# Loading one weight matrix in another order of partitions: a source walked as 16 sets of rows instead of 128 rows

## The chip, the cores and the metric

The kernel runs on one core of a Trainium2 chip. The metric is the device time of one execution in microseconds (us). A run over 1.5% above the fastest of its kernel would be called slow.

The names used: HBM is the large memory, SBUF the on-chip memory, whose leading axis is 128 partitions. PE (TensorE) multiplies matrices, DVE is the vector engine, and SyncE and ScalarE issue loads. The 16 DMA engines that carry the loads are meant wherever the text says that an engine reads or writes rows.

## The reference

Two independent problems, A and B, of the same shape, each one step of attention for a decoder with a cache. The results are put side by side.

```python
B, Sq, D = 2, 1, 576;  Hq, Hkv, Sk, Dh = 32, 16, 16384, 128      # bf16 throughout
W = min(4096, max(256, Sk // 4))                                  # 4096: the window
q = (x @ wq).reshape(B, Sq, Hq, Dh)          # wq is 576 x 4096, 4.72 MB
k, v = the last W rows of k_cache, v_cache   # 2 x 16 x 4096 x 128 each, 33.6 MB each
o = softmax(q k^T * Dh**-0.5) v
out = o.reshape(B, Sq, Hq * Dh) @ wo
```

Almost all of the work is reading 153 MB from HBM. wq of A, which the change touches, is 3% of it.

## The kernel before

The kernel holds wq in SBUF as 128 partitions of 18,432 elements (36,864 B), and partition p holds piece p of the flat matrix. Nine half rows of wq lie in one piece, so x has to be spread over the partitions in the same way: element i of x that belongs to a half row goes to the partition that holds that half row. The DVE does this with 32 x 32 transposes. The matmuls then contract over the partitions, and the order of the partitions does not matter as long as wq and x agree.

```python
wq_dma = {}
for P in range(NPROB):
    def f_wq(e, P=P):
        src = probs[P][3].rearrange("a b -> (a b)").rearrange("(p f) -> p f", p=128)
        return e.dma_start(ringf[:, P * QW:(P + 1) * QW], src).then_inc(wq_sem[P], 16)
    wq_dma[P] = dma_op("sp", wq_sem[P], 1, f_wq, [], "wq%d" % P)
# ... (cut) in turn_x(P):
    def f_xT(e, P=P):
        for k in range(4):
            last = e.transpose(xU[32 * k:32 * k + 32, P, :, 4 * P:4 * P + 32],
                               xs[:, P * 2 * D:(P + 1) * 2 * D].rearrange("p (c t) -> p t c", t=NU)[:, :, 32 * k:32 * k + 32])
# ... (cut) the matmuls of A wait for wq_dma[0] and the transposes; the caches are loaded behind wq:
    src = src_t[b, 4 * g:4 * g + 4, Sk - W:Sk, :].rearrange("k (r j) d -> r k j d", j=KJ)   # 32 x 4 rows of 32,768 B
    e.dma_start(ring[:, r, c0 * 128:c1 * 128], src[:, :, c0:c1, :].rearrange("r k j d -> r k (j d)"))
```

SyncE issues all the large loads in one order: wq of A, wq of B, then the caches into a ring of four slots, and wo among the caches. The load of wq of A is the first thing in this queue. (The small loads of x are issued by ScalarE.)

Of the kernel before, what the change touches and what calls it, by code (L numbers as in the profile page):

```python
# [62 lines left out]
def build_kernel(nc, probs, out):  # L63
# [5 lines left out]
    Bb, _one, D = x0.shape  # L69
# [18 lines left out]
    NU = (2 * D) // 128  # L88
    QW = NU * UW
# [3 lines left out]
    with es:  # L93
# [50 lines left out]
        ringf = ring[:].rearrange("p r f -> p (r f)")  # L144
# [3 lines left out]
        xU = pTf[:, 0:XW].rearrange("p (g u w) -> p g u w", g=NPROB, u=NU)  # L148
# [3 lines left out]
        xs = xt[0:32, 1, 0:NPROB * 2 * D]  # L152
# [8 lines left out]
        wq_sem = [sem("wq%d" % P) for P in range(NPROB)]  # L161
# [7 lines left out]
        def dma_op(eng, sem_h, n_dmas, fn, deps, tag):  # L169
            op = S.add(eng, fn, deps, tag)  # L170
            dma_count[sem_h] = dma_count.get(sem_h, 0) + 16 * n_dmas
            op.dma = (sem_h, dma_count[sem_h])
            return op
# [9 lines left out]
        wq_dma = {}  # L183
        for P in range(NPROB):
            def f_wq(e, P=P):
                src = probs[P][3].rearrange("a b -> (a b)").rearrange("(p f) -> p f", p=128)
                return e.dma_start(ringf[:, P * QW:(P + 1) * QW], src).then_inc(wq_sem[P], 16)
            wq_dma[P] = dma_op("sp", wq_sem[P], 1, f_wq, [], "wq%d" % P)

        pool = lambda fn, deps, tag: S.add("pool", fn, deps, tag)  # L190
# [30 lines left out]
        def turn_x(P):  # L221
            d_xs = dve(lambda e, P=P: e.tensor_tensor(xs[0:4, P * 2 * D:(P + 1) * 2 * D].rearrange("p (i t) -> p i t", t=2),  # L222
                                                      x4[:, P, :].unsqueeze(2).broadcast_to([4, D, 2]),
                                                      hmask[:, 0:2].unsqueeze(1).broadcast_to([4, D, 2]), ALU.mult),
                       [x_dma[P], d_hm, p_zx], "xs%d" % P)

            def f_xT(e, P=P):
                for k in range(4):
                    last = e.transpose(xU[32 * k:32 * k + 32, P, :, 4 * P:4 * P + 32],
                                       xs[:, P * 2 * D:(P + 1) * 2 * D].rearrange("p (c t) -> p t c", t=NU)[:, :, 32 * k:32 * k + 32])  # L230
                return last
            d_xT.append(dve(f_xT, [d_xs, p_zxU], "xT%d" % P))

# [520 lines left out]
        for op in order:  # L754
            have = seen[op.eng]
            need = {}
            for d in op.deps:
# [3 lines left out]
                k = id(s_h)  # L761
# [62 lines left out]
```

## Time and profile before

| | before |
|---|---|
| time, median of 2 | 363.21 us |
| DMA queue busy, of 16 engines' span | 98.7% |
| PE, DVE busy | 66%, 60% |
| mean rate | 424 GB/s |
| one wq row (36,864 B) on one DMA engine | 1.364 us, 27.0 GB/s |

From the profile's page of the kernel before: the busy tenths of PE and of the DMA engines and the rate in 40 slices of 9 us, and the share of the queue.

```profile
PE   0497787666485747662596675567776875668695
...
DMA  8999999999999999999999999999999999999996
GB/s 327 457 435 406 460 408 446 424 431 438 417 453 408 457 404 428 444 431 431 435 420 444 417 449 410 440 431 438 424 442 412 449 417 429 435 435 431 417 412 256
...
q1 hardware_dynamic: 6196, 153.10, 98.7%
```

DMA never falls below 9 tenths between the first slice and the last, at about 430 GB/s: the time is the bytes. The next busiest engine, PE, stands at 66%. So a microsecond lost or won in the queue at the start should move the end by about a microsecond.

From the timeline of the kernel before (start, duration, engine, what; in brackets the idle time ahead and what ended it): the issues of the first loads, the transposes of x and the first matmuls on A's and on B's wq.

```profile
0.80 0.39 SPq L187 DMA_DIRECT2D ring<-in_A_wq_dram  x1
1.25 0.41 SPq L187 DMA_DIRECT2D ring<-in_B_wq_dram  x1
...
9.63 2.78 DVE L229 STREAM_TRANSPOSE pT<-xt 32x288 bf16<-32x288 bf16 x4
...
14.20 0.61 PE L279 MATMUL ot<-ring,pT 128*32 128x512 bf16 x1 [14.20 <-DMA ring<-in_A_wq_dram]
...
25.07 0.39 PE L279 MATMUL ot<-ring,pT 128*32 128x512 bf16 x1 [0.79 <-DMA ring<-in_B_wq_dram]
```

A's wq is there at 14.2 us and B's at 25.1 us, 10.9 us later. A's x is turned by 12.4 us, so PE waits for the load and not for x.

The trace also holds one record per DMA packet, here a row of wq: its start and how long it took. It doesn't say which engine moved it. Taking the 256 wq rows in the order of their start, sixteen at a time (sixteen are in flight in 164 of 174 instants, one every 0.1 us, so I take a turn as one row per engine), the first turn takes 1.97 us on average, the second 1.37, and all others 1.364.

### The profile page before, as it was taken

Reading aid. Unit: us, or ns where it says so; the run is one execution under the profiler, and the core shown is the slowest. Engines: PE = TensorE matmul, PEld = TensorE weight load, DVE = VectorE, ACT = ScalarE, POOL = GpSimd, SP = SyncE. Lnnn points to the kernel's source line nnn. Section 1 sums busy time; section 2 is a strip of 40 time slices with the busy share of each in tenths; the row PEclk is TensorE's granted clock in tenths of the full one; section 3 lists DMA queues with packets and bytes.
Section 4 is the critical chain, followed back from the end, with each engine's and each line's share of the span. In section 5 each row is a group of like instructions: output and inputs, shape, how many; then the busy total and the mean of one; then the engine's idle time right before and its main releaser. Section 6 shows DMA issues by size and latency. Waiting matters only on the chain.

```text
span 361.8 us, 2625 instructions
## 1 busy us (share of the span) xinstructions
PE 240.2 (66%) x1292; PEld 57.2 (16%) x927; DVE 218.7 (60%) x150; ACT 46.0 (13%) x78; POOL 24.3 (7%) x84
## 2 busy tenths in 40 slices
PE   0497787666485747662596675567776875668695
PEld 0000111112111201111121121112112121112222
DVE  1901898495929591934909585682927776674622
ACT  1002100040023000500005000500005000500500
POOL 4200101100010001000010000100010001000000
PEclk9999698969988996888788796888688796868969
DMA  8999999999999999999999999999999999999996
GB/s 327 457 435 406 460 408 446 424 431 438 417 453 408 457 404 428 444 431 431 435 420 444 417 449 410 440 431 438 424 442 412 449 417 429 435 435 431 417 412 256
DMA packets 6227, 153.26 MB, mean 424 GB/s; under 512 B 700, under 2 KB 840, under 8 KB 1224
## 3 DMA queue, kind: packets, MB, share of 16 engines
q1 hardware_dynamic: 6196, 153.10, 98.7%
q8 instruction: 8, 0.13, 0.1%
q14 instruction: 3, 0.02, 0.0%
q10 hardware_dynamic: 20, 0.01, 0.0%
HBM read 153.10 MB, written 0.00 MB: 423 GB/s over the span
## 4 chain that ended last, share of the span: by engine, by line
DMA 48%; DVE 26%; PE 16%; issue 8%; ACT 1%; POOL 0%; SPq 0%
DMA ring<-in_B_k_cache_dram 17%; DVE xt L433 16%; DMA ring<-in_A_k_cache_dram 13%; DMA ring<-in_B_v_cache_dram 9%; DMA ring<-in_B_wq_dram 7%; PE st L264 5%; PE st L459 5%; DMA wob<-in_B_wo_dram 3%; PE pj L264 2%; DVE oR L566 2%; DVE mx L467 2%; DVE pT L506 2%; DVE tmp L559 2%; PE ot L536 2%; PE pj L618 1%
## 5 line engine op out<-in xcount | busy, mean ns | idle before, releaser
L459 PE MATMUL st<-xt,zq 128*128 128x512 bf16 x256 | 124.1, 485 | 86.1 <-DVE xt L433 86.1
L433 DVE STREAM_TRANSPOSE xt<-ring 128x4096 f32<-128x4096 f32 x32 | 141.5, 4427 | 28.0 <-DMA ring<-in_A_k_cache_dram 18.8
L264 PE MATMUL st<-xt,zq 128*128 128x512 bf16 x256 | 122.7, 479 | 0.0
L497 ACT ACTIVATE pR<-st,bias 128x512 bf16<-128x512 f32 x32 | 40.0, 1414 | 222.9 <-DVE bias L490 222.9
L459 PEld LDWEIGHTS st<-xt,zq 128*128 128x128 bf16 x256 | 29.4, 115 | 210.1 <-issue 107.7
L536 PE MATMUL ot<-ring,pT 128*32 128x512 bf16 x512 | 32.6, 396 | 3.9 <-DMA ring<-in_B_v_cache_dram 3.9
L490 DVE SCALAR_TENSOR_TENSOR bias<-vmask,tb,offm 128x4 f32<-128x4 f32 x8 | 1.8, 223 | 43.0 <-PE tb L487 43.0
L520 DVE TENSOR_REDUCE ssum<-tb 128x2 f32<-128x8 f32 x8 | 1.3, 162 | 36.0 <-PE tb L517 36.0
L425 POOL TENSOR_TENSOR zq<-qs,bmask 128x64 bf16<-128x64 bf16 x32 | 8.7, 293 | 168.1 <-PE st L264 145.8
L506 DVE STREAM_TRANSPOSE pT<-pR 128x2048 bf16<-128x2048 bf16 x8 | 18.4, 2303 | 0.8 <-ACT pR L497 0.7
L279 PE MATMUL ot<-ring,pT 128*32 128x512 bf16 x18 | 7.6, 421 | 15.0 <-DMA ring<-in_A_wq_dram 14.2
L559 DVE SCALAR_TENSOR_TENSOR tmp<-ot,rsb,dmask 128x512 f32<-128x512 f32 x16 | 11.5, 719 | 7.9 <-PE ot L536 7.9
L566 DVE TENSOR_REDUCE oR<-tmp 128x128 f32<-128x512 f32 x15 | 15.6, 1042 | 0.5
L536 PEld LDWEIGHTS ot<-ring,pT 128*32 128x32 bf16 x512 | 12.4, 99 | 19.6 <-DMA ring<-in_B_v_cache_dram 5.5
L618 PE MATMUL pj<-wob,oM 128*2 128x288 bf16 x48 | 12.7, 299 | 0.0
L264 PE MATMUL pj<-wob,oM 128*2 128x288 bf16 x48 | 12.7, 299 | 0.0
L264 PE MATMUL pj<-ring,pT 128*32 128x512 bf16 x36 | 11.9, 416 | 0.0
L467 DVE TENSOR_REDUCE mx<-st 128x2 f32<-128x1024 f32 x8 | 9.7, 1213 | 0.1
L497 ACT ACTIVATION_READ_ACCUMULATOR pR<-st,bias 128x1 f32 x32 | 8.8, 276 | 0.0
L264 PE MATMUL st<-ring,pT 128*32 128x512 bf16 x18 | 7.3, 407 | 0.0
L222 DVE TENSOR_TENSOR xt<-xt,hmask 4x1152 bf16<-4x1152 bf16 x2 | 2.7, 1349 | 6.7 <-DMA xt<-in_A_x_dram 6.7
L469 POOL TENSOR_TENSOR mv<-mx,v 128x2 f32<-128x2 f32 x8 | 1.6, 195 | 75.8 <-DVE mx L467 75.8
(68 smaller groups left out, 75.6 us busy)
## 6 DMA issues: line engine op xcount, KB each, us to landing
ring<-in_A_k_cache_dram SPq DMA_DIRECT2D x8, 4096.0 KB, 24.3
ring<-in_A_v_cache_dram SPq DMA_DIRECT2D x8, 4096.0 KB, 29.9
ring<-in_B_k_cache_dram SPq DMA_DIRECT2D x8, 4096.0 KB, 27.0
ring<-in_B_v_cache_dram SPq DMA_DIRECT2D x7, 4096.0 KB, 29.8
ring<-in_A_wq_dram SPq DMA_DIRECT2D x1, 4608.0 KB, 13.3
ring<-in_B_wq_dram SPq DMA_DIRECT2D x1, 4608.0 KB, 23.8
wob<-in_A_wo_dram SPq DMA_DIRECT2D x2, 2304.0 KB, 28.3
wob<-in_B_wo_dram SPq DMA_DIRECT2D x1, 2304.0 KB, 27.4
```

The lines of the kernel that those rows point to most:

```text
L264: return e.add_instruction(mybir.InstMatmult(name=nc.get_next_instruction_name(), engine=mybir.EngineType.PE, ins=[e.lower_ap(mv_), e.lowe ...
L279: last = e.matmul(QB[c], wt, mv_, start=first, stop=True, skip_group_check=True)
L425: last = e.tensor_tensor(dst, src, msk, ALU.mult)
L433: Xop[(t, jh)] = dve(lambda e: e.transpose(xt[:, jh, :].bitcast(FP32).rearrange("p (kp x kt) -> p x kp kt", kp=2, kt=2), ring[:, r, jh * H ...
L459: last = e.matmul(ob, wt, mv_, start=first, stop=True, skip_group_check=True)
L467: ch[(G, "max")] = dve(lambda e: e.tensor_reduce(mx[:], st[:, :].rearrange("p (x t) -> p t x", t=2), AX.X, ALU.max), [Sop[(2 * G + 1, 1)]] ...
L497: last = e.activation(pR[:].rearrange("p (x k) -> p k x", k=4)[:, kv, :], st[:, :].rearrange("p (x t) -> p t x", t=2)[:, kv % 2, :], ACTF.Exp,
L506: pT_op[G] = dve(lambda e: e.transpose(pT[:, v, :].rearrange("p (w j q) -> p j w q", w=4, q=8), pR[:].rearrange("p (j w q) -> p j w q", w= ...
L536: last = e.matmul(OTB[32 * c:32 * c + 32, :], pT[:, v, base + 32 * c:base + 32 * c + 32], ring[:, r, jj * 128:(jj + 4) * 128], start=rd == ...
L559: evac_op[i] = dve(lambda e: e.scalar_tensor_tensor(tv, o, rsb[:, v, b:b + 1], dm, ALU.mult, ALU.mult), deps, "ev%d" % i)
L566: ch[(G, "red%d" % b)] = dve(lambda e: e.tensor_reduce(oR[:, b, :], tmp[:].rearrange("p (j d) -> p d j", j=4), AX.X, ALU.add), [evac_op[i] ...
L618: last = e.matmul(PJ[h], oM[:, j, :], mv_, start=start and j == 0, stop=True, skip_group_check=True)
```

## The change

In the new order partition 8r+m holds piece 16m+r. The intent is that sixteen neighbouring pieces are read at a time, eight such sets one after the other. Only A's load, the first in the queue, is changed. x is turned to match.

```diff
-                src = probs[P][3].rearrange("a b -> (a b)").rearrange("(p f) -> p f", p=128)
-                return e.dma_start(ringf[:, P * QW:(P + 1) * QW], src).then_inc(wq_sem[P], 16)
+                src, dst = probs[P][3].rearrange("a b -> (a b)"), ringf[:, P * QW:(P + 1) * QW]
+                src = src.rearrange("(m r f) -> r m f", m=8, r=16) if P == 0 else src.rearrange("(p f) -> p f", p=128)
+                return e.dma_start(dst, src).then_inc(wq_sem[P], 16)
 ...
-                    last = e.transpose(xU[32 * k:32 * k + 32, P, :, 4 * P:4 * P + 32],
-                                       xs[:, P * 2 * D:(P + 1) * 2 * D].rearrange("p (c t) -> p t c", t=NU)[:, :, 32 * k:32 * k + 32])
+                    xv = xs[:, P * 2 * D:(P + 1) * 2 * D]
+                    if P == 0:
+                        xv = xv.rearrange("p (m k a t) -> p k t a m", m=8, k=4, a=4)[:, k]
+                        xo = xU[32 * k:32 * k + 32, P, :, 4 * P:4 * P + 32].rearrange("p t (a m) -> p t a m", m=8)
+                    else:
+                        # ... (cut) the old access of B, written differently
+                    last = e.transpose(xo, xv)
```

The source is now walked as 16 x 8 rows. The destination is still 128 partitions in order. The bytes, the number of rows and the size of a row are as before.

More of the change, by code (lines that the diff above doesn't have):

```diff
@@ L228, in f_xT @@
                 for k in range(4):
-                    last = e.transpose(xU[32 * k:32 * k + 32, P, :, 4 * P:4 * P + 32],
-                                       xs[:, P * 2 * D:(P + 1) * 2 * D].rearrange("p (c t) -> p t c", t=NU)[:, :, 32 * k:32 * k + 32])
+                    xv = xs[:, P * 2 * D:(P + 1) * 2 * D]
[3 more added lines that the diff above has]
+                    else:
+                        xv = xv.rearrange("p (k c t) -> p k t c", k=4, c=32)[:, k]
+                        xo = xU[32 * k:32 * k + 32, P, :, 4 * P:4 * P + 32]
+                    last = e.transpose(xo, xv)
                 return last
```

## The prediction

> **What bounds the kernel.** The 16 DMA engines. On the profile's page the DMA queue that SyncE issues is busy for 98.7% of 16 engines' span, at 424 GB/s on average; DMA stands at 9 tenths in 38 of 40 slices. In the trace's packet records a 36,864 B row of wq takes an engine 1.364 us and a 32,768 B row of the caches 1.213 us: 27.0 GB/s an engine, 432 GB/s for 16. From the first packet (1.8 us) to the last weight packet (359.2 us) the packets' time divided by 16 is 357.1 us of 357.4. In the steady part bytes set the time.
>
> Only the start is different. The two wq loads come first. Of the 256 wq rows all take 1.364 us except the first one on each engine: those 16 take 1.77 to 2.35 us, 2.0 on average (one second packet takes 1.51). That sums to 0.61 us per engine, the only loss that the change can address.
>
> **What the change does.** Same bytes, rows, packets and issues. Partition 8r+m gets piece 16m+r. [...] 1.364 us per row says that the old order costs nothing[...]. So the new order can take only part of the 0.61 us,[...] the fastest first packet is still 0.40 us over.
>
> The transposes of A's x read with stride 288 B instead of 18 B; output, block count and size stay. Before: 4 at 0.686 us each, done at 12.4 us, while A's wq lands at 14.2 (timeline). Even at twice the time they would delay only A's projection by 1 us; its end (24.1 us) releases a cache load that the queue needs only at about 34.8 us. B's transposes and PE's work are unchanged.
>
> **Critical path.** The queue never runs dry, so time saved at the start passes nearly one for one. Expected saving 0.25 us, at most 0.6.
>
> **Predicted time: 362.9 us, range 362.2 to 363.6.** Faster by over 2%: 1%. Within 2%: 88%. Slower by over 2%: 11%.
>
> **Signs.** Right: A's wq lands at 13.5 to 14.3 us; its 128 packets still take 1.364 us except the first 16, and those average 1.7 to 2.0; B's wq lands within 0.6 us of 25.1; the end moves alike; A's transposes stay near 0.69 us each.
>
> **What would make it wrong.** The split over the engines. [...] The new source has a slowest dimension of 16[...]. [...] An estimate: rows at 2.7 us instead of 1.364, eight per engine, so wq A lands about 10.9 us later, and all after it: 374 us. The cache loads (slowest source dimension 32, four heads inside) run at full rate, which speaks against it but does not rule it out. The sign: wq A packets well above 1.364 us, and GB/s in the first two slices halved.

363.2 us for the kernel before, less an estimated saving of 0.25 us (out of the 0.61 us by which the first rows exceed 1.364), is the 362.9 us. In the second sum, that of the danger, 2.7 us are twice 1.364, eight rows make 8 x 1.364 = 10.9 us more, and 363.2 + 10.9 = 374 us.

## The result

| | before | after |
|---|---|---|
| time, median of 2 | 363.21 us | 375.00 us |
| ratio | | 1.0325 (95%: 1.0274 to 1.0376) |
| the same once more, 4 runs beside 7 of before | 363.30 us | 374.62 us, 1.0313 (1.0297 to 1.0328) |
| wq row after the first turn, A | 1.365 us | 2.85 us |
| wq row after the first turn, B | 1.364 us | 1.37 us |

A ratio is the mean time of one kernel's fast runs over the mean of the other's in the same rounds, so it isn't quite the ratio of the medians in the table.

The kernel is 11.8 us slower, where a range of 362.2 to 363.6 us had been given. The same lines of the profile's page, after (a slice is now 9.3 us):

```profile
PE   0028859946685765648278585748476677665885
...
DMA  8999999999999999999999999999999999999995
GB/s 190 202 296 422 407 449 442 401 445 445 417 428 443 428 419 442 420 440 428 424 445 426 421 442 435 431 426 424 442 428 424 435 435 431 419 438 435 414 419 242
...
q1 hardware_dynamic: 6196, 153.10, 98.6%
```

This is the line to remember. The engines are as busy as before, 8 tenths in the first slice and 9 in all others but the last, yet they move 190 and 202 GB/s in the first two slices where they moved 327 and 457. From the fourth slice on the rate is the old one. The busy share of a DMA engine says that it has a packet in hand and not that the packet is moving at full speed.

The timeline after:

```profile
0.80 0.68 SPq L188 DMA_DIRECT2D ring<-in_A_wq_dram  x1
...
1.54 0.57 SPq L188 DMA_DIRECT2D ring<-in_B_wq_dram  x1
...
10.39 2.76 DVE L237 STREAM_TRANSPOSE pT<-xt 32x288 bf16<-32x288 bf16 x4
...
26.15 0.61 PE L286 MATMUL ot<-ring,pT 128*32 128x512 bf16 x1 [26.15 <-DMA ring<-in_A_wq_dram]
...
37.08 0.39 PE L286 MATMUL ot<-ring,pT 128*32 128x512 bf16 x1 [1.70 <-DMA ring<-in_B_wq_dram]
```

A's wq is there 12.0 us later, and B's 12.0 us later; nothing is given back afterwards. A's transposes cost what they did, 2.76 us for four. The issue takes 0.68 us instead of 0.39; why is not shown (the issue of B, whose source is plain as before, takes 0.57 us instead of 0.41).

The packet records of A's wq, sixteen at a time (my grouping; us):

```
turn              1      2      3      4      5      6      7      8
before, mean    1.968  1.373  1.364  1.364  1.364  1.364  1.364  1.364
after, mean     2.431  2.872  2.876  2.870  2.698  2.863  2.876  2.869
```

The loss adds up. The packets' time per engine in A's load went from 11.52 to 22.36 us (+10.83), in B's load from 10.91 to 11.40 (+0.49, its first turn), and the first packet started at 2.26 us instead of 1.82 (+0.44). The sum is 11.76 us; the first row of the caches starts 11.78 us later (35.91 against 24.13).

One detail will matter: the fifth turn is a little faster, 2.70 us. An engine has eight rows if each takes one per turn, so something changes for it after four. What changes is not shown.

### The profile page after: what moved, and what is told of

It reads as the page before. It is cut to its first block, busy times and chain, and to the rows that moved or that the text cites. A ratio compares the mean times of both kernels' runs of the same rounds, so it can differ in the third digit from the quotient of the medians.

```text
span 373.9 us, 2626 instructions
## 1 busy us (share of the span) xinstructions
PE 235.2 (63%) x1293; PEld 56.8 (15%) x927; DVE 218.5 (58%) x150; ACT 45.9 (12%) x78; POOL 23.3 (6%) x84
## 4 chain that ended last, share of the span: by engine, by line
DMA 49%; DVE 25%; PE 16%; issue 7%; ACT 1%; POOL 0%; SPq 0%
DMA ring<-in_B_k_cache_dram 16%; DVE xt L440 15%; DMA ring<-in_A_k_cache_dram 12%; DMA ring<-in_B_wq_dram 9%; DMA ring<-in_B_v_cache_dram 9%; PE st L271 5%; PE st L466 5%; DMA wob<-in_B_wo_dram 3%; PE pj L271 2%; DVE oR L573 2%; DVE mx L474 2%; DVE pT L513 2%; DVE tmp L566 2%; ACT pR L504 1%; PE pj L625 1%
## 5 line engine op out<-in xcount | busy, mean ns | idle before, releaser
L466 PE MATMUL st<-xt,zq 128*128 128x512 bf16 x256 | 121.1, 473 | 89.1 <-DVE xt L440 89.1
L271 PE MATMUL st<-xt,zq 128*128 128x512 bf16 x256 | 119.8, 468 | 0.0
L543 PE MATMUL ot<-ring,pT 128*32 128x512 bf16 x512 | 33.7, 406 | 7.1 <-DMA ring<-in_B_v_cache_dram 7.1
L286 PE MATMUL ot<-ring,pT 128*32 128x512 bf16 x18 | 7.3, 406 | 27.8 <-DMA ring<-in_A_wq_dram 26.1
L566 DVE SCALAR_TENSOR_TENSOR tmp<-ot,rsb,dmask 128x512 f32<-128x512 f32 x16 | 11.5, 719 | 11.9 <-PE ot L543 11.8
L543 PEld LDWEIGHTS ot<-ring,pT 128*32 128x32 bf16 x512 | 12.7, 100 | 23.2 <-DMA ring<-in_B_v_cache_dram 9.6
L286 PEld LDWEIGHTS ot<-ring,pT 128*32 128x32 bf16 x18 | 1.8, 100 | 42.1 <-DMA ring<-in_A_wq_dram 26.1
```

The lines of the kernel that those rows point to most:

```text
L271: return e.add_instruction(mybir.InstMatmult(name=nc.get_next_instruction_name(), engine=mybir.EngineType.PE, ins=[e.lower_ap(mv_), e.lowe ...
L286: last = e.matmul(QB[c], wt, mv_, start=first, stop=True, skip_group_check=True)
L466: last = e.matmul(ob, wt, mv_, start=first, stop=True, skip_group_check=True)
L543: last = e.matmul(OTB[32 * c:32 * c + 32, :], pT[:, v, base + 32 * c:base + 32 * c + 32], ring[:, r, jj * 128:(jj + 4) * 128], start=rd == ...
L566: evac_op[i] = dve(lambda e: e.scalar_tensor_tensor(tv, o, rsb[:, v, b:b + 1], dm, ALU.mult, ALU.mult), deps, "ev%d" % i)
```

## The experiments

The change may have altered four things at once: the order in which HBM is read, the form of the load (two levels), which partitions are written at the same time, and the turning of x. Theory P is a supposition, the risk that the prediction had named: two engines that write certain partitions at the same time slow each other to half the rate. Why they would, and which engine writes which partitions, no run shows. What the runs can test is the consequence, that the time of a row depends on where the load writes. Rivals: H, neighbouring reads collide in HBM; D, a two-level source is slow whatever it writes; S, only the start of the queue is sensitive.

Every run was timed in three rounds beside the kernel before, whose median was 363.1 to 363.3 us each time. All runs passed the comparison with the reference. That says little here: the first experiment below feeds A's projection the wrong x and passes too, so the comparison doesn't see the order of wq. That the changed kernel is right follows from the algebra: partition 8(4k+a)+m holds piece 16m+4k+a, whose half row u is column 144m+36k+9a+u of x, which is what the new access reads.

### x_only: turn x, leave the load

```diff
-  src = src.rearrange("(m r f) -> r m f", m=8, r=16) if P == 0 else src.rearrange("(p f) -> p f", p=128)
+  src = src.rearrange("(p f) -> p f", p=128)
```

> Only x is turned for the new order, A's wq is loaded in the old one; wrong result on purpose. All theories: 363.2 us, within 0.4, and the four transposes of A at 2.8 us together: the turning of x costs nothing.

Measured: 363.12 us, ratio 0.9997 (0.9981 to 1.0014), A's four transposes 2.76 us together. The whole loss is in the load.

### m4: 32 x 4 rows instead of 16 x 8, meant for neighbouring reads

```diff
-  src.rearrange("(m r f) -> r m f", m=8, r=16) if P == 0
+  src.rearrange("(m r f) -> r m f", m=4, r=32) if P == 0
-  xv.rearrange("p (m k a t) -> p k t a m", m=8, k=4, a=4)    # and m=8 in xo
+  xv.rearrange("p (m k a t) -> p k t a m", m=4, k=4, a=8)    # and m=4 in xo
```

> A's wq in a related order: partition 4r+m gets piece 32m+r, so the slowest source dimension is 32 instead of 16 (x turned to match, right result). [...] Theory P[...]: rows of wq A take 1.36 us after the first, A lands near 14 us, total 363 us, within 0.5. Rival H (HBM: sixteen engines reading neighbouring pieces in step collide on the read side): rows near 2.8 us, total near 375. Rival D (any two-level source order makes slow descriptors): near 375.

Measured: 363.39 us, ratio 1.0004 (0.9989 to 1.0019). Rows after the first turn take 1.368 us on average. In the windows from 4 to 12 and 12 to 24 us (columns: stretch and length, busy time and number of instructions of PE, PE's weight loads, DVE, ACT and POOL, granted clock, DMA share, GB/s), first the changed kernel, then m4:

```profile
4.00:12.00 8.00, 0.00 (x0) 0.00 (x0) 2.93 (x4) 0.00 (x0) 1.27 (x3) 1.00 1.08 222
12.00:24.00 12.00, 0.00 (x0) 0.00 (x0) 6.11 (x13) 0.00 (x0) 1.15 (x5) 1.00 0.94 197
```

```profile
4.00:12.00 8.00, 0.00 (x0) 0.00 (x0) 5.37 (x11) 0.00 (x0) 1.88 (x7) 1.00 1.03 443
12.00:24.00 12.00, 9.18 (x31) 0.94 (x8) 4.17 (x5) 0.00 (x0) 1.65 (x3) 1.00 1.03 442
```

The last two numbers of each line are the ones to read: the share is about 1 in both, the rate doubles. m4 has a two-level source, so D falls. It was also built to read pieces 36 KB apart at the same time; if it does, this speaks against H. The intended gain is hardly to be seen in it: the first turn of A's rows takes 1.92 us, against 1.97 before and 2.03 in x_only, which loads A just as before does. The issue took 0.61 us and the queue started 0.39 us later.

### m2: 64 x 2 rows

> Slowest source dimension 64: partition 2r+m gets piece 64m+r, x to match. Theory P: as with 32,[...] rows 1.36 us, total 363 to 363.6; the longer issue of a two-level source (0.68 against 0.39 us) starts the queue about 0.3 to 0.4 us later.

The edit is that of m4 with m=2, r=64 and a=16. Measured: 363.67 us, 1.0013 (0.9998 to 1.0028); rows at 1.365 us, the first packet at 2.22 us against 1.82. 64 and 32 as the slowest dimension are harmless (1.365 and 1.368 us per row), 16 is not (2.85 us).

### halves: the old order, but two loads of 64 partitions

```diff
-  return e.dma_start(ringf[:, P * QW:(P + 1) * QW], src).then_inc(wq_sem[P], 16)
+  for p0, p1 in ([(0, 64), (64, 128)] if P == 0 else [(0, 128)]):
+      last = e.dma_start(ringf[p0:p1, P * QW:(P + 1) * QW], src[p0:p1, :]).then_inc(wq_sem[P], 16)
```

> Old order (piece p on partition p), but A's wq as two loads, partitions 0 to 63, then 64 to 127; right result. The source is plain[...]. Theory P:[...] rows take 2.7 to 2.9 us, A lands near 25.5 us, total 374 to 376. Rivals H and D: nothing about the source has changed except its start, rows 1.36 us, total 363 to 364.

Measured: 375.29 us, 1.0332 (1.0316 to 1.0347), turns after the first 2.74 to 2.88 us on average. This is the loss of the change without its order: piece p on partition p, a plain one-level source, x as it was. So the order and the form of the source are not needed for it. By theory P the place of the writes is what the two have in common; for halves it is known (64 of the 128 partitions at a time), for the changed kernel the records don't show it.

### mid16 and mid: 64 partitions from 32 on

```diff
-  src = ...; return e.dma_start(dst, src)
+  mid = src[32:96, :].rearrange("(m r) f -> r m f", m=4, r=16)      # in mid: src[32:96, :]
+  for p0, p1, sv in [(32, 96, mid), (0, 32, src[0:32, :]), (96, 128, src[96:128, :])]:
+      last = e.dma_start(dst[p0:p1, :], sv).then_inc(wq_sem[P], 16)
   # in mid16, x is turned to match on partitions 32 to 95
```

> A's wq as three loads: partitions 32 to 95 with a source of slowest dimension 16 (16 x 4[...]), then 0 to 31 and 96 to 127 in plain order; x matches, right result. Theory P:[...] the first 64 rows take 1.36 us (first ones about 2) and the last 64 rows, 32 partitions over 16 engines, take 2.7 to 2.9 us; A lands near 20 us, total 368 to 370. Rivals H and D: the reverse, the first 64 rows near 2.8 us and the last 64 at 1.36; about the same total, so the packets decide.

> As mid16 but with the old order: partitions 32 to 95 as one plain load of 64 rows, then 0 to 31, then 96 to 127; right result. [...] first 64 rows 1.36 us, total 369.7 as mid16. [...] all 128 rows 2.7 to 2.9 us, total about 375.

(mid's text gives two possible outcomes, the first 64 rows at 1.36 us or all 128 at 2.7 to 2.9. Each stood for a way of sharing the 64 rows out among the engines. No record names an engine.)

Measured: mid16 369.73 us, 1.0180 (1.0165 to 1.0196); mid 370.19 us, 1.0186 (1.0169 to 1.0203). The turns of A's rows, mean us (turns 1 to 4 are partitions 32 to 95, turns 5 to 8 the two loads of 32):

```
turn            1      2      3      4      5      6      7      8
mid16         1.639  1.390  1.382  1.376  2.596  2.858  2.706  2.845
mid           1.977  1.365  1.364  1.442  2.522  2.831  2.648  2.844
```

Packets decide here, as the total was to be about the same under all theories. mid16 loads partitions 32 to 95 with a source whose slowest dimension is 16, built like the change's to read sixteen neighbouring pieces at a time, and after its first turn it runs at 1.376 to 1.390 us per row. A source in that order and the 16 are not slow in themselves. mid shows that a plain load of 64 partitions, which in halves took 2.9 us per row, takes 1.364 us when it starts 32 partitions further on. Only the place where the rows are written differs in kind. The windows from 4 to 7 us, first halves, then mid:

```profile
4.00:7.00 3.00, 0.00 (x0) 0.00 (x0) 0.00 (x0) 0.00 (x0) 1.26 (x3) 1.00 0.97 197
```

```profile
4.00:7.00 3.00, 0.00 (x0) 0.00 (x0) 0.62 (x1) 0.00 (x0) 1.27 (x3) 1.00 1.00 431
```

H falls here, as far as a source built so is also read so; with m4, D falls twice.

The table shows one thing more. mid16's first turn took 1.64 us and mid's 1.98. In shift16b and shift16 below, which differ from each other in the same way, it was 2.21 and 2.53. Each pair writes the same partitions, and only the order of reading and the form of the source differ, so the source built to read sixteen neighbouring pieces may well shorten the first turn by about 0.3 us. These are single profiles; before and x_only, with the same load of A, differ by 0.06 us.

### shift28: the 64 partitions moved down by four

```diff
-  (32, 96, mid16's source), (0, 32), (96, 128)
+  (28, 92, the same 16 x 4 source from row 28), (92, 128), (0, 28)
```

> A's wq in three loads: first partitions 28 to 91 with a 16 x 4 source as in mid16[...], then 92 to 127 and 0 to 27; x not turned for it, wrong result on purpose. [...] Theory own[...]: of the rows that start before 7 us about an eighth take 2.7 to 2.9 us and the others 1.36 (first ones up to 2). Theory pace[...]: all rows of that load near 2.8 us. Total 366 to 380, from the loads behind it.

(What told the two theories apart: I supposed that one pair of engines is in each other's way here. By own only its rows are slow, by pace all rows.)

Measured: 377.66 us in total, 1.0396 (1.0380 to 1.0411), set by the awkward loads of 36 and 28 rows behind it (from 7 to 13 us 265 GB/s, against 419 from 4 to 7). The first load is the experiment. Its rows that started between 3.7 and 7 us, when the first turn is over, beside the same count for other runs:

```
run        first load of A's wq          rows started  at most 1.5 us  over 2.3 us
m4         128 partitions, 32 x 4             37            37             0
mid        32 to 95, plain                    35            35             0
mid16      32 to 95, 16 x 4                   38            36             0
shift28    28 to 91, 16 x 4                   34            31             3
shift16b   16 to 79, 16 x 4                   17             0            17
halves     0 to 63, plain                     16             0            16
after      128 partitions, 16 x 8             16             0            16
```

Moving the load down by four partitions slows three of 34 rows and no others. If two of sixteen engines ran at half the rate, they would finish 1 row where the other fourteen finish 14, so about 1 in 15 by number, or two of 34 (an estimate from row times of 2.7 and 1.364 us). The three slow rows took 2.43, 2.68 and 2.71 us, the latter two nearly twice 1.364, while the rows beside them took 1.364. They lie on two chains, as two engines would give: the 2.43 us row starts at 4.33 us and the 2.71 us row at 6.76 us, where it ends; the 2.68 us row is the other chain. This fits theory P with one pair; which partitions the slow rows were written to is not shown. (Two rows of mid16 took between 1.5 and 1.7 us.)

### shift16 and shift16b: 64 partitions from 16 on

> Old order, A's wq in three loads: partitions 16 to 79, then 80 to 127, then 0 to 15. Theory P[...]:[...] of the first 64 rows 32 take 1.36 us (the first ones about 1.8) and 32 take 2.7 to 2.9 us, at the same time. Under any theory by the source or the number of partitions all 64 would be alike. Total between 368 and 376, from the two smaller loads behind it.

> As shift16, but the first load (partitions 16 to 79) has the 16 x 4 source of shift28; x not turned for it, wrong result on purpose. What is open: shift16 slowed all 64 rows[...]. Theory split (a plain load of 64 rows from partition 16 is split over the engines in another way than I supposed): here 32 of the first 64 rows take 1.36 us (the first ones up to 2.3) and 32 take 2.7 to 2.9. Theory crowd[...]: all 64 rows near 2.85 us again, total near 383 as shift16.

(By crowd, the engines that I supposed to be out of each other's way are held back too.)

In shift16 the edit is that of halves with (16, 80), (80, 128), (0, 16), in shift16b that of shift28 with the same three stretches. Measured: 382.97 us, 1.0542 (1.0527 to 1.0558), and 382.88 us, 1.0540 (1.0522 to 1.0558). In both, all rows of the first load after the first turn took 2.74 to 2.89 us. My expectation for shift16 failed: only 32 of the 64 rows should have been slow. Another split of a plain 64-row load (theory split) is out as well: mid, which is plain, runs at the full rate, and shift16b, with the 16 x 4 source, is as slow as shift16. The windows from 4 to 7 us, first shift28, then shift16b:

```profile
4.00:7.00 3.00, 0.00 (x0) 0.00 (x0) 0.00 (x0) 0.00 (x0) 1.26 (x3) 1.00 1.05 419
```

```profile
4.00:7.00 3.00, 0.00 (x0) 0.00 (x0) 0.00 (x0) 0.00 (x0) 1.27 (x3) 1.00 1.01 210
```

From partition 28 on, 31 of 34 rows took at most 1.5 us; from 16 on, none did. So theory P as I had written it, that engines are slowed only in their own pairs, is not the whole account: half of the rows from 16 on were to stay fast by it. That half was my estimate and rested on a reason that no run shows. Where between 28 and 16 this begins, and why, stays open. It doesn't touch the changed kernel, where all turns after the first take 2.70 to 2.88 us on average.

### b_only: the change on B's load, second in the queue

```diff
-  ... if P == 0      # in the load and in the turning of x
+  ... if P == 1
```

> The change made to B's wq instead of A's (x of B turned to match). Theory P: it is the shape of the load that costs, wherever it stands in the queue, so B's 128 rows take 2.7 to 2.9 us, A's stay at 1.36, B lands 11 to 12 us late, total 374.5 to 375.5. Rival S (the engines collide only because they start the queue in step; after A's load they have drifted apart): B's rows near 1.36 us, total 363 to 364.

Measured: 375.53 us, 1.0341 (1.0325 to 1.0356). A's rows take 1.36 us again, B's 2.66 to 2.93 after their first turn. S falls: B's first sixteen rows started spread over 13.26 to 14.22 us, most of the 1.36 us that a row takes, and B was slowed just the same.

### m16: 8 x 16 rows

> Slowest source dimension 8: partition 16r+m gets piece 8m+r, x to match. Theory P[...]: only 8 engines are used[...]: 16 rows of 2.7 to 2.9 us on each engine, 46 us for the load, about 35 us late, total 397 to 400, DMA share near half in that stretch. [...]

The edit is that of m4 with m=16, r=8 and a=2. Measured: 415.09 us, 1.1419 (1.1399 to 1.1438). The direction was right and the size was not; A's wq was there at 66.6 us where 46 us for the load had been expected, so 48 or so. The timeline of m16:

```profile
66.56 0.61 PE L286 MATMUL ot<-ring,pT 128*32 128x512 bf16 x1 [66.56 <-DMA ring<-in_A_wq_dram]
```

The packets show why. Up to about 34 us sixteen wq rows are in flight, and from 36 to 57 us only eight at a time, one turn every 4.1 us: by these counts eight engines carry all of A's wq, sixteen rows each, and the other eight go ahead to B's wq and the first cache load. But rows of both take 3.7 to 4.1 us, three times 1.364, and the cache rows beside them 3.6 us, three times 1.213. I had counted only the pairs within A's load and not the engines that ran ahead. That these are the reason is a guess: no run here tests it, and why a row takes three times as long and not twice stays open. The rows of A are also faster in every fourth turn after the first (3.72 to 3.78 us against 4.06 to 4.12), as the fifth turn of the changed kernel was (2.70 us against 2.86 to 2.88). What changes after four rows is not shown.

## Why the prediction was wrong

**What bounds the kernel: right.** The delay of A's load (11.78 us at the first cache row) arrived at the end nearly whole (11.8 us in the medians).

**"Expected saving 0.25 us, at most 0.6": wrong for this kernel.** The saving assumed that the first packets were slow in part because of the order in which they read, which was not shown. In the changed kernel A's first turn rose from 1.97 to 2.43 us. In m4, which was built to read neighbouring pieces and keeps 1.368 us per row, it fell by 0.05 us, which is within the scatter. mid16 beside mid and shift16b beside shift16 suggest that about 0.3 us can be had with a source built so that all sixteen pieces are neighbours; that stays unproven. A later start of the queue (0.44 us in the changed kernel, 0.39 in m4, 0.40 in m2), which would use up such a gain, had been left out. That the longer issue causes it is not shown: b_only issues A's load in 0.40 us, and A's wq was there at 15.16 us instead of 14.20.

**The step that failed: "The cache loads (slowest source dimension 32, four heads inside) run at full rate, which speaks against it".** The prediction saw the danger, worked out its size, put 374 us on it, and then gave 11% to all times over 2% slower, with a similar load that ran well as its argument. What failed is its cost of a row: the 1.364 us that A's rows were to keep after the first became 2.85 us, while cache rows of 32 x 4 kept 1.22 us. The two loads aren't alike; what in their shapes makes the difference is not shown, as the records name neither engine nor partition. What the runs show is that for these 128 rows a slowest dimension of 64 or 32 keeps the full rate (1.365 and 1.368 us per row), 16 halves it (2.85 us), and with 8 the rows took 3.7 to 4.1 us and for a while only eight were in flight; and that 64 plain rows run at half or full rate by where they are written (2.9 us from partition 0 in halves, 1.364 us from 32 in mid).

**The size in "What would make it wrong": right.** It had estimated 2.7 us per row and 10.9 us; measured were 2.85 us and 10.83 us in A's rows. That the sums agree so closely is partly luck: a row after the first turn lost 1.48 us and not 1.36, and a row of the first turn only 0.46. With 0.44 us from the later start and 0.49 us in B's first turn the loss is 11.76 us.

**The turning of x: right.** 2.76 us after, 2.78 before; x_only cost nothing.

No version beat the kernel before: m4 and m2, the two with 1.37 us per row in a new order, are 0.2 to 0.6 us slower by their medians, within or at the edge of their intervals.

## What to carry to other kernels

When you rearrange the source of a load, its rate can change though bytes, rows and destination stay: 128 partitions and sixteen busy engines don't yet mean full rate (190 and 202 GB/s at 8 and 9 tenths busy in the changed kernel). For rows of 36,864 B into 128 partitions, a slowest dimension of 32, 64 or 128 gave 1.36 to 1.37 us per row here and 16 gave 2.85; a 64-partition load gave 1.364 us at 32 to 95 and 2.9 at 0 to 63. Keep to the shapes that were fast, and check GB/s in the trace, not the busy share. If a prediction names a risk with a definite size, compare the two shapes that it turns on before you give it a low chance because a similar shape did well.
